# Linear attention, gated convolution and channel mixing on one core: the order of the first 40 microseconds, and eight weights' shifts moved from VectorE to ScalarE

## The chip, the cores and the metric

The kernel runs on one core of one Trainium2 chip. The metric is device time in microseconds (us), lower is better. The time before is 793.02 us, the median of three runs (792.64, 793.02 and 794.86). The engines are named as the profile names them: PE is TensorE, DVE is VectorE, ACT is ScalarE, POOL is GpSimd, SP is SyncE, which here only issues the transfers (DMAs).

## The reference

Eight sequences of 576 positions, 8 heads of 64, so rows of 512. Three stages follow each other:

```
q_s = softmax(q over its 64 features);  k_s = softmax(k over the 576 positions)
kv  = einsum('bhsd,bhde->..', k_s, v)          # 64x64 per head
x   = q_s @ kv                                  # rows of 512
gate = sigmoid(causal convolution of x, 5 taps, per channel)
x   = ((gate * (x @ w_val)) @ w_out)
xk  = mu_k*x + (1-mu_k)*x_prev;  xr = mu_r*x + (1-mu_r)*x_prev
out = sigmoid(xr @ w_r) * (relu(xk @ w_k)**2 @ w_v)
```

The five weight matrices and the convolution's taps come as float64. The kernel reads each number as two 32-bit words and makes the float32 from them.

## The kernel before, in words

The 4608 rows are handled in 12 blocks of 384. Every block runs attention (`px`), the product with w_val (`pv`), with w_out (`py`), with w_r (`racc`), with w_k (`ph`) and with w_v (`vacc`). Blocks 2 to 11 follow a fixed table; the first two blocks, the loading of all weights and the first key-value sums are issued in the order of a written list, `FRONT`. A scheduler in the framework then places the instructions of the list on each engine, so an engine's order is near to the list's but not the same; it is fixed when the program is built. Each engine works through its own queue strictly in that order.

What the front does, by the list's names:

- `lk`, `lv`, `lwval0`, ... load keys, values and weights; `qload0.0` and `qload1.0` load the two halves of the first block's query (4 heads each, tile `came`). `wval0`, `wout0`, ... turn a loaded weight chunk (tile `raw`, 128x512 pairs of words) into float32 (tile `whole`); the function is `decode`: one ACT instruction rescales the high word (L154), one DVE instruction shifts the low word right (L155), one DVE instruction joins them (L156).
- For the first key-value round: `max0` is the running maximum over the keys (tile `pm`, DVE L320 and L322); `turn0` transposes it on PE (`pmT`) and reduces it on DVE (`m1`, printed as `m`); `exp0` spreads the maximum on PE (`mx`), subtracts it (DVE, `kt`) and takes the exponential (ACT, `kt`); `vcopy0` copies the values into place (ACT, `vt`); `mm0` multiplies keys by values on PE (`kvacc`) and divides by the sums (DVE, `den`, `kvf`). `max1` to `mm1` do it for the second round, heads 4 to 7.
- `qexp0.0`, `qnorm0.0` are the softmax of the query's first half on DVE and ACT (`qm`, `qt`, `qs`); `xturn` transposes it on PE (`pq`), `xq` copies it out (ACT, `q`), `x0.0` to `x3.0` multiply it with `kvf` (PE, `px`) and copy the result (ACT, `xf`). The chunks x0 and x1 need the first half of the query and the first round, x2 and x3 the second half and the second round.
- `gate` is the convolution: one ACT and four DVE instructions for each chunk, then a tanh (ACT). `gf` multiplies it to `pv`.
- `consts` turns the convolution's taps and the mixing factors (`cwt`, `pc`, `cw`, `pm`, `mus`).
- `heat1`, `heat2`, `heat6`, `heat3`, `heat0`, `heat7` are eight transposes of the identity each on PE; nothing reads their result.

`pmT`, `mx`, `pq` and `kvacc` share the two PSUM banks of the pool `ps_t`; `pv`, `racc`, `vacc` and `heat` use the three of `ps_acc`.

Of the kernel before, what the change touches and what calls it, by code (L numbers as in the profile page):

```python
# [62 lines left out]
CONV_ON_TENSOR = ()  # L63

# [4 lines left out]
def tile_linear_attention_gated_conv_channel_mix(  # L69
# [21 lines left out]
    P = 128  # L91
# [59 lines left out]
    def decode(raw, out):  # L151

        low, high = raw[:, :, 0], raw[:, :, 1]
        nc.scalar.activation(f32(high), f32(high), AF.Prelu, scale=2.0 ** -112, alpha=2.0 ** 32)  # L154
        nc.vector.tensor_scalar(out=low, in0=low, scalar1=29, scalar2=None, op0=ALU.logical_shift_right)  # L155
        nc.vector.scalar_tensor_tensor(  # L156
            out=out.bitcast(U32), in0=high, scalar=3, in1=low, op0=ALU.logical_shift_left, op1=ALU.bitwise_or
        )
# [8 lines left out]

    cts = {}
# [9 lines left out]
    def turn_consts():  # L178
        raw, mut = cts["x"]
        t = scratch("cwt")[0:NTAP * NC, 0:P]  # L180
        decode(raw, t)
        pc = ps_t.tile([P, 512], F32, tag="t", name="pc")
        nc.tensor.transpose(pc[:, 0:NTAP * NC], t, f32(ident[0:NTAP * NC, 0:NTAP * NC]))
        nc.scalar.copy(cw, pc[:, 0:NTAP * NC])
        pm = ps_t.tile([P, 512], F32, tag="t", name="pm")
        nc.tensor.transpose(pm[:, 0:2 * NC], mut, f32(ident[0:2 * NC, 0:2 * NC]))
        ups = mus.rearrange("p x c -> p (x c)")
        nc.scalar.copy(ups[:, 0:2 * NC], pm[:, 0:2 * NC])
        nc.vector.tensor_scalar(
            out=ups[:, 2 * NC:4 * NC], in0=ups[:, 0:2 * NC], scalar1=-1.0, scalar2=1.0, op0=ALU.mult, op1=ALU.add  # L190
        )
# [28 lines left out]
    def decode_weight(n):  # L220
        w, at = CHUNKS[n]
        whole[w, at] = place(F32, "whole")
        decode(raws[n], whole[w, at])
# [50 lines left out]
    latest = {}  # L274
# [37 lines left out]
    def v_copy(st):  # L312
        nc.scalar.copy(st["v"][:, :, 0:NS4, 0:D], st["dense"])

    def kv_max(st):
        kt = st["k"]
        whole_pm = scratch("pm")
        pm = whole_pm[:, 0:HR * D]
        one = pm.rearrange("p (h d) -> p h d", d=D)
        nc.vector.tensor_max(one, kt[:, :, 0, :], kt[:, :, 1, :])  # L320
        for x in range(2, NST):
            nc.vector.tensor_max(one, one, kt[:, :, x, :])  # L322
        st["pm"] = whole_pm

    def kv_turn(st):
        pm, n = st["pm"], HR * D // P
        pmT = ps_t.tile([P, 512], F32, tag="t", name="pmT")
        for j in range(n):
            nc.tensor.transpose(pmT[:, j * P:(j + 1) * P], pm[:, j * P:(j + 1) * P], f32(ident))
        m1 = odd.tile([P, n], F32, tag="m1", bufs=2, name="m1")  # L330
        nc.vector.tensor_reduce(
            out=m1, in_=pmT[:, :n * P].rearrange("p (j t) -> p j t", j=n), axis=AX.X, op=ALU.max
        )
        st["m1"] = m1
# [33 lines left out]
    def kv_exp(st):  # L368

        kt, m1, n = st["k"], st["m1"], HR * D // P  # L370
        mx = ps_t.tile([P, 512], F32, tag="t", name="mx")
        for j in range(n):
            nc.tensor.transpose(mx[:, j * P:(j + 1) * P], m1[:, j:j + 1].to_broadcast([P, P]), f32(ident))
        nc.vector.tensor_sub(
            kt, kt, mx[:, :n * P].rearrange("p (h o d) -> p h o d", o=1, d=D).to_broadcast([P, HR, NST, D])
        )
        nc.scalar.activation(kt, kt, AF.Exp)

    def kv_mm(st):
# [3 lines left out]
        acc = ps_t.tile([P, 512], F32, tag="t", name="kvacc")  # L383
# [68 lines left out]
    def q_exp(st, h=slice(0, H)):  # L452
        n = h.stop - h.start
        qt = st["qt"][:, :, h, :]
        src = st["came"].rearrange("p h t d -> p t h d")[:, :, h, :] if "came" in st else qt
        qm = odd.tile([P, NT * n], F32, tag=f"qm{n}", bufs=1, name="qm").rearrange("p (t h) -> p t h", t=NT)
        nc.vector.tensor_reduce(out=qm, in_=src, axis=AX.X, op=ALU.max)
        nc.vector.tensor_sub(qt, src, qm.rearrange("p t (h o) -> p t h o", o=1).to_broadcast([P, NT, n, D]))
        nc.scalar.activation(qt, qt, AF.Exp)

    def q_norm(st, h=slice(0, H)):
# [136 lines left out]
    def x_chunk(st, i, c):  # L598
# [4 lines left out]
        for o, n, b, s in segs:  # L603
# [5 lines left out]
            with behind if o == 0 else nullcontext():  # L609
                passes(to, tuple(a[:, c, :] for a in kv), tuple(a[:, at] for a in st["q", c]), True, True)  # L610
        xv = padded(i, HALO, "xf", 2, "xf") if i else padded(i, HALO, "xf", NC, "xf", first)
# [8 lines left out]
        else:  # L620
            nc.scalar.copy(data, px[:, :T].rearrange("p (g t) -> p g t", g=g))
# [31 lines left out]
    def x_gate(st, i, c):  # L653
# [10 lines left out]
        nc.scalar.activation(gx(gate), data, AF.Copy, scale=tap(c, HALO))  # L664
        for sh in range(1, NTAP):
            nc.vector.scalar_tensor_tensor(  # L666
                out=gx(gate), in0=xv[:, :, HALO - sh:HALO - sh + L], scalar=tap(c, HALO - sh),
                in1=gx(gate), op0=ALU.mult, op1=ALU.add,
            )
# [11 lines left out]
    def main_steps(i, xs):  # L681
# [68 lines left out]
        def mix(c, key, mu, om, tag, pair):  # L750
# [3 lines left out]
            nc.vector.scalar_tensor_tensor(  # L754
# [135 lines left out]
    todo_front = {"cload": load_consts, "consts": turn_consts, "kvsplit": kv_split}  # L890
# [73 lines left out]
```

## Time and profile before

| | |
|---|---|
| median of three runs | 793.02 us (792.64 to 794.86) |
| the profiled execution | 793.22 us, of which the span is 791.4 us |
| PE busy in the span | 780.5 us (99%) |
| DVE busy | 600.1 us (76%) |
| ACT busy | 477.5 us (60%) |
| DMA, mean of 16 engines, 0 to 10 and 10 to 20 us | 0.79 and 1.08 |

The profile shows one execution. A timeline row is a start, a length, an engine, a source line, an operation, out<-in, sizes and how many instructions it merges; in brackets stands how long the engine sat idle before it and what released it. A product of float32 tiles is two records on PE, so `px x4` is two products. Neighbouring instructions of one engine overlap a little, so the step from start to start is often shorter than the length. `heat` and the first `pmT` stand at the start of the span, `px` at 19.02 us is the first product of the first block.

### The profile page before, as it was taken

The page shows a single profiled execution, that of the slowest core. Times are in us where ns is not written, and L with a number is a line of the kernel's source. Part 1 is how long each engine was busy: PE and PEld are TensorE (multiplying, and loading weights), DVE is VectorE, ACT ScalarE, POOL GpSimd, SP SyncE. Part 2 cuts the span into 40 slices and gives each one's busy share as a digit, 9 for nine tenths or more (in the row PEclk, how much of TensorE's full clock was granted, in tenths as well). Part 3 has the DMA queues.
Part 4 walks back from the last instruction along what each step waited for, and adds up shares of the span by engine and source line. Part 5 has one row for each costly group of instructions (what it writes and reads, how often), then busy time and mean ns, then how long its engine had stood idle before and what let it go on. Part 6 is the DMA issues. An engine that isn't in the chain of part 4 may idle for free.

```text
span 791.4 us, 12490 instructions
## 1 busy us (share of the span) xinstructions
PE 780.5 (99%) x4426; PEld 686.3 (87%) x4426; DVE 600.1 (76%) x1190; ACT 477.5 (60%) x969; POOL 64.8 (8%) x224
## 2 busy tenths in 40 slices
PE   6999999999999999999999999999999999999998
PEld 5545679999999989999999999999999999999996
DVE  7998889988788588678787678678978848755611
ACT  4667678546746665754763772763774665573542
POOL 2130001000001011100000110100000100100000
PEclk9999999999999999999999999999999999999999
DMA  9787220134133112312441411411522202101001
GB/s 314 241 273 237 60 80 1 41 104 139 35 117 102 46 46 93 89 41 82 113 100 61 128 41 48 140 37 51 141 66 82 73 15 80 59 23 39 2 1 41
DMA packets 91708, 68.88 MB, mean 87 GB/s; under 512 B 48738, under 2 KB 83454, under 8 KB 91646
## 3 DMA queue, kind: packets, MB, share of 16 engines
q1 hardware_dynamic: 91600, 68.06, 28.5%
q8 instruction: 35, 0.57, 0.3%
q14 instruction: 27, 0.22, 0.1%
q10 hardware_dynamic: 46, 0.02, 0.0%
HBM read 51.54 MB, written 16.53 MB: 86 GB/s over the span
## 4 chain that ended last, share of the span: by engine, by line
PE 95%; DMA 2%; DVE 1%; ACT 1%; SPq 1%; issue 0%; ACTq 0%
PE ph L551 26%; PE vacc L551 26%; PE racc L551 12%; PE pv L551 12%; PE py L551 12%; PE px L551 4%; PE kvacc L387 2%; DMA raw<-in_moe_w_val_dram 1%; DMA raw<-in_moe_w_k_dram 1%; DVE gate L666 1%; DMA kt<-in_k_dram 1%; PE pq L578 0%; SPq L310 0%; DVE whole L156 0%; DVE gf L717 0%; SPq L304 0%
## 5 line engine op out<-in xcount | busy, mean ns | idle before, releaser
L666 DVE SCALAR_TENSOR_TENSOR gate<-xf,cw,gate 128x384 f32<-128x384 f32 x192 | 116.3, 615 | 4.1 <-ACT gate L664 1.0
L551 PE MATMUL ph<-xkh,wk_hi 128*128 128x384 f32 x352 | 118.4, 336 | 0.0
L551 PE MATMUL ph<-xkl,wk_hi 128*128 128x384 f32 x352 | 118.2, 336 | 0.0
L551 PE MATMUL ph<-xkh,lower 128*128 128x384 f32 x352 | 117.8, 336 | 0.0
L780 ACT ACTIVATE rf<-ph 128x384 f32<-128x384 f32 x96 | 46.8, 488 | 97.9 <-PE ph L551 97.5
L544 DVE TENSOR_TENSOR kl<-rf,kh 128x384 fp32r<-128x384 f32 x88 | 48.9, 556 | 74.7 <-ACT kh L543 74.5
L551 PE MATMUL vacc<-wv_hi,kh 128*128 128x512 f32 x264 | 103.9, 394 | 0.0
L551 PE MATMUL vacc<-lower,kh 128*128 128x512 f32 x264 | 103.4, 392 | 0.0
L551 PE MATMUL vacc<-wv_hi,kl 128*128 128x512 f32 x264 | 103.3, 392 | 0.0
L543 ACT CAST gh<-gf 128x384 fp32r<-128x384 f32 x44 | 22.6, 513 | 104.0 <-DVE gf L717 104.0
L551 PEld LDWEIGHTS ph<-xkh,wk_hi 128*128 128x128 f32 x352 | 66.1, 188 | 2.4 <-ACT xkh L543 0.2
L551 PEld LDWEIGHTS ph<-xkh,lower 128*128 128x128 f32 x352 | 66.1, 188 | 2.3
L551 PEld LDWEIGHTS ph<-xkl,wk_hi 128*128 128x128 f32 x352 | 66.1, 188 | 0.0
L754 DVE SCALAR_TENSOR_TENSOR xm<-yf,mus,xm 128x384 f32<-128x384 f32 x96 | 56.2, 612 | 11.8 <-ACT xm L753 11.5
L551 PE MATMUL py<-gh,wout_hi 128*128 128x384 f32 x176 | 60.0, 341 | 0.0
L551 PE MATMUL pv<-xh,wval_hi 128*128 128x384 f32 x176 | 59.3, 337 | 0.0
L551 PE MATMUL py<-gl,wout_hi 128*128 128x384 f32 x176 | 58.9, 337 | 0.0
L551 PE MATMUL pv<-xl,wval_hi 128*128 128x384 f32 x176 | 58.9, 335 | 0.0
L551 PEld LDWEIGHTS vacc<-wv_hi,kl 128*128 128x128 f32 x264 | 49.5, 188 | 10.8 <-DVE kl L544 0.3
L551 PE MATMUL pv<-xh,lower 128*128 128x384 f32 x176 | 58.9, 334 | 0.0
L551 PE MATMUL py<-gh,lower 128*128 128x384 f32 x176 | 58.8, 336 | 0.0
L753 ACT ACTIVATE xm<-yf,mus 128x384 f32<-128x384 f32 x96 | 56.4, 615 | 3.0 <-DVE xrl L544 1.6
(152 smaller groups left out, 1696.6 us busy)
## 6 DMA issues: line engine op xcount, KB each, us to landing
out_dram<-rs SPq DMA_DIRECT2D x36, 256.0 KB, 2.2
kt<-in_k_dram SPq DMA_DIRECT2D x16, 512.0 KB, 4.4
vt<-in_v_dram SPq DMA_DIRECT2D x56, 128.0 KB, 3.9
turned<-sq SPq DMA_DIRECT2D x36, 192.0 KB, 1.9
qT<-turned SPq DMA_DIRECT2D x72, 96.0 KB, 2.2
qn<-in_q_dram SPq DMA_DIRECT2D x24, 192.0 KB, 3.4
raw<-in_moe_w_k_dram SPq DMA_DIRECT2D x8, 512.0 KB, 5.2
raw<-in_moe_w_v_dram SPq DMA_DIRECT2D x8, 512.0 KB, 5.2
```

Of the source, the lines that this page charges most:

```text
L387: nc.tensor.matmul(acc[e * D:(e + 1) * D, x * VW:(x + 1) * VW], lhsT=kt[:, 2 * x + e, s, :], rhs=st["v"][:, 2 * x + e, s, :], start=(s == ...
L543: latest["round"] = nc.scalar.copy(pair[0], a)
L544: latest["split"] = nc.vector.tensor_sub(pair[1], a, f32(pair[0]))
L551: latest["matmul"] = nc.tensor.matmul(po, lhsT=left[a], rhs=right[b], start=start and x == 0, stop=stop and x == len(m) - 1)
L666: nc.vector.scalar_tensor_tensor(out=gx(gate), in0=xv[:, :, HALO - sh:HALO - sh + L], scalar=tap(c, HALO - sh), in1=gx(gate), op0=ALU.mult ...
L753: nc.scalar.activation(gx(xf), yv[:, :, 0:L], AF.Copy, scale=om[:, c:c + 1])
L754: nc.vector.scalar_tensor_tensor(out=gx(xf), in0=yv[:, :, 1:], scalar=mu[:, c:c + 1], in1=gx(xf), op0=ALU.mult, op1=ALU.add)
L780: nc.scalar.activation(rf, ph[:, :T], AF.Relu)
```

## The change

Four things are altered, all in the first two blocks. The list `FRONT` is in another order: the first values are loaded ahead of the second keys, the constants are turned first, `max1` and `turn1` stand ahead of `xturn0.0`, and `exp1`, `wval1` and `vcopy1` ahead of `qexp1.0`. For eight weight chunks (w_val and w_out) `decode` shifts the low word on ACT instead of DVE, reading its top byte. The first round's `kvacc` and the second round's `pmT` take banks of `ps_acc` instead of `ps_t`. And many instructions are held, by `after(...)`, until a named other one in the issue order; the scheduler may not place them before it.

```diff
 FRONT = (
-    "qload.0 qload0.0 lk0 cload lwval0 lwval1 lk1 lv0 lv1 lwval2 qload1.0 lwout0 lwval3 lwout1 lwr0 max0 turn0 exp0 "
-    "lwout3 lwr1 heat1 heat2 lwout2 qexp0.0 wval0 vcopy0 mm0 heat6 qnorm0.0 heat3 heat0 heat7 xturn0.0 xq0.0 x0.0 "
-    "xturn1.0 xq1.0 x1.0 max1 qexp1.0 turn1 exp1 vcopy1 consts wval1 qnorm1.0 V0.0 mm1 gate0.0 V1.0 xturn2.0 xq2.0 "
+    "qload.0 qload0.0 lk0 cload consts lwval0 lv0 lk1 lwval1 lv1 lwval2 qload1.0 lwval3 lwout0 lwout1 lwr0 max0 turn0 "
+    "exp0 lwout3 lwr1 heat1 heat2 lwout2 qexp0.0 wval0 vcopy0 mm0 heat6 qnorm0.0 heat3 heat0 heat7 max1 turn1 xturn0.0 "
+    "xq0.0 xturn1.0 xq1.0 x0.0 exp1 wval1 x1.0 vcopy1 others qexp1.0 V0.0 mm1 qnorm1.0 gate0.0 V1.0 xturn2.0 xq2.0 "
...
+ON_SCALAR = "wval0 wval1 wval2 wval3 wout0 wout1 wout2 wout3".split()
+BEHIND = {
+    "wval0": ("mus", "m1.0"), "wval1": ("kexp.0", "m1.1"), "wval2": ("qexp.1", "kvf.1"), "wval3": ("qexp.1", "kvf.1"),
...
+        with after(act):
+            nc.scalar.activation(f32(high), f32(high), AF.Prelu, scale=2.0 ** -112, alpha=2.0 ** 32)
+            if on_scalar:
+                fourth = raw.rearrange("p n w -> p (n w)").bitcast(U8).rearrange("p (n e) -> p n e", e=8)[:, :, 3]
+                latest["shifted"] = nc.scalar.activation(low, fourth, AF.Copy, scale=2.0 ** -5, bias=-31.0 / 64)
+        with after(vec):
+            if not on_scalar:
+                nc.vector.tensor_scalar(out=low, in0=low, scalar1=29, scalar2=None, op0=ALU.logical_shift_right)
...
+    def bank_of(st, name, x):
+        if st is rounds[x]:
+            return ps_acc.tile([P, 512], F32, tag="acc", name=name)
+        return ps_t.tile([P, 512], F32, tag="t", name=name)
...
-        pmT = ps_t.tile([P, 512], F32, tag="t", name="pmT")
+        pmT = bank_of(st, "pmT", 1)
...
-        nc.vector.tensor_reduce(
-            out=m1, in_=pmT[:, :n * P].rearrange("p (j t) -> p j t", j=n), axis=AX.X, op=ALU.max
-        )
+        with after("kvf.0" if x == 1 else None):
+            latest[f"m1.{x}"] = nc.vector.tensor_reduce(
...
-        acc = ps_t.tile([P, 512], F32, tag="t", name="kvacc")
+        acc = bank_of(st, "kvacc", 0)
...
-        nc.vector.tensor_reduce(out=qm, in_=src, axis=AX.X, op=ALU.max)
+        with after("sub.1" if h.start else "cwt" if h.stop == HR else "sub.2"):
+            nc.vector.tensor_reduce(out=qm, in_=src, axis=AX.X, op=ALU.max)
```

On PE, the program's first rows before, from the identity's transposes to the first product of the first block (`m_177` and `m_320` are the first and second round's maxima, `kvf_118` the sums of sequence 0):

```order
L887 MATMUL heat<-ident 128x128 x16
L329 MATMUL pmT<-ident,pm 128x128 x2
L887 MATMUL heat<-ident 128x128 x6
L373 MATMUL mx<-ident,m_177 128x128 x2
L887 MATMUL heat<-ident 128x128 x26
L387 MATMUL kvacc<-vt,kt 64x65 x20
L578 MATMUL pq<-ident,qt 128x128 x6
L329 MATMUL pmT<-ident,pm 128x128 x2
L551 MATMUL px<-q,kvf_118 128x384 x2
```

And the same stretch of PE now (the lines have other numbers, `m_187` and `m_302` are the two maxima):

```order
L929 MATMUL heat<-ident 128x128 x2
L201 MATMUL pc<-ident,cwt 128x20
L204 MATMUL pm<-ident,mut 128x8
L929 MATMUL heat<-ident 128x128 x14
L359 MATMUL pmT<-ident,pm 128x128 x2
L405 MATMUL mx<-ident,m_187 128x128 x2
L419 MATMUL kvacc<-vt,kt 64x65 x20
L929 MATMUL heat<-ident 128x128 x32
L359 MATMUL pmT<-ident,pm 128x128 x2
L612 MATMUL pq<-ident,qt 128x128 x6
L585 MATMUL px<-q,kvf_118 128x384
```

The 32 transposes of the identity that stood ahead of `kvacc` (6 and 26) stand behind it, between it and the second round's `pmT` and the query's `pq`.

On DVE, the stretch around the second round's maximum and the query's second half before:

```order
L457 TENSOR_REDUCE qm<-came 128x12
L399 TENSOR_TENSOR kvf_118<-kvacc,den 64x2x64 x2
L458 TENSOR_TENSOR qt<-came,qm 128x3x256
L331 TENSOR_REDUCE m_320<-pmT 128x2
L155 TENSOR_SCALAR raw<-raw 128x512 x2
L374 TENSOR_TENSOR kt_125<-kt_125,mx 128x1280
L466 TENSOR_REDUCE qs<-qt 128x12
L189 TENSOR_SCALAR mus<-mus 128x8
L666 SCALAR_TENSOR_TENSOR gate<-xf,cw,gate 128x384
L467 TENSOR_SCALAR qs<-qs 128x12
```

And now:

```order
L431 TENSOR_TENSOR kvf_118<-kvacc,den 64x2x64 x2
L362 TENSOR_REDUCE m_302<-pmT 128x2
L176 SCALAR_TENSOR_TENSOR whole<-raw 128x512
L406 TENSOR_TENSOR kt_125<-kt_125,mx 128x1280
L211 TENSOR_SCALAR mus<-mus 128x8
L490 TENSOR_REDUCE qm<-came 128x12
L491 TENSOR_TENSOR qt<-came,qm 128x3x256
L705 SCALAR_TENSOR_TENSOR gate<-xf,cw,gate 128x384 x3
L426 TENSOR_SCALAR den<-kvacc 128x2
L500 TENSOR_REDUCE qs<-qt 128x12
L427 RECIPROCAL den<-den 128x2
L705 SCALAR_TENSOR_TENSOR gate<-xf,cw,gate 128x384
```

The two passes of the query's second half (`qm`, `qt`) stood ahead of the second maximum `m_320` and stand behind the subtraction `kt_125`; the sum `qs` stands behind three taps of the gate. The last pass of that half, `qt<-qt,qs`, follows seven rows further.

On ACT, from the taps' word to the copies of the query, before:

```order
L154 ACTIVATE cwraw<-cwraw 20x128
L154 ACTIVATE raw<-raw 128x512 x2
L459 ACTIVATE qt<-qt 128x3x256
L313 COPY vt<-dense 128x4x4x64
L377 ACTIVATE kt<-kt 128x1280
L313 COPY vt_126<-dense 128x4x4x64
L154 ACTIVATE raw<-raw 128x512
L590 COPY q<-pq 128x384 x2
```

And now, where L172 is the shift that came from DVE:

```order
L169 ACTIVATE cwraw<-cwraw 20x128
L202 COPY cw<-pc 128x20
L206 COPY mus<-pm 128x8
L169 ACTIVATE raw<-raw 128x512
L172 ACTIVATE raw<-raw 128x512
L335 COPY vt<-dense 128x4x4x64
L492 ACTIVATE qt<-qt 128x3x256
L409 ACTIVATE kt<-kt 128x1280
L169 ACTIVATE raw<-raw 128x512
L172 ACTIVATE raw<-raw 128x512
L624 COPY q<-pq 128x384 x2
```

One weight instead of two is decoded ahead of the first `kt`, and the copy of the second values (`vt_126`) and the third weight no longer stand ahead of the query's copies.

## Rows read from the trace of the kernel before

**Rows 1.** Page: the span; the chain that ended last, by engine.
```profile
span 791.4 us, 12490 instructions
...
PE 95%; DMA 2%; DVE 1%; ACT 1%; SPq 1%; issue 0%; ACTq 0%
```

**Rows 2.** Windows: busy per engine (instructions), granted clock, DMA share, GB/s.
```profile
20.00:30.00 10.00, 9.76 (x71) 5.77 (x70) 9.56 (x22) 8.26 (x16) 0.88 (x5) 1.00 0.71 256
30.00:40.00 10.00, 10.00 (x32) 5.61 (x31) 9.38 (x19) 5.30 (x10) 1.23 (x2) 1.00 0.77 222
...
60.00:760.00 700.00, 700.00 (x4036) 629.65 (x4035) 541.11 (x1070) 431.09 (x886) 50.59 (x177) 1.00 0.25 74
```

**Rows 3.** Timeline of PE, 0 to 60 us.
```profile
3.34 3.67 PE L887 MATMUL heat<-ident 128*128 128x128 f32 x16 [3.34 <-DVE ident L162]
9.13 0.69 PE L329 MATMUL pmT<-ident,pm 128*128 128x128 f32 x2 [2.12 <-DVE pm L322]
...
10.90 0.63 PE L373 MATMUL mx<-ident,m 128*128 128x128 f32 x2
11.32 3.67 PE L887 MATMUL heat<-ident 128*128 128x128 f32 x26
15.13 1.39 PE L387 MATMUL kvacc<-vt,kt 128*64 128x65 f32 x40
...
17.57 0.55 PE L578 MATMUL pq<-ident,qt 128*128 128x128 f32 x3 [0.57 <-ACT q L590]
...
19.02 1.56 PE L551 MATMUL px<-q,kvf 128*128 128x384 f32 x4
...
28.12 0.82 PE L578 MATMUL pq<-ident,qt 128*128 128x128 f32 x6
29.18 1.56 PE L551 MATMUL px<-q,kvf 128*128 128x384 f32 x4 [0.24 <-ACT q L590]
...
49.77 7.99 PE L551 MATMUL racc<-whole,xm 128*128 128x512 f32 x18 [0.28 <-ACT yf L745]
```

**Rows 4.** Timeline of PE, 12 to 12.5 and 13 to 13.5 us.
```profile
11.75 1.06 PE L887 MATMUL heat<-ident 128*128 128x128 f32 x4
...
12.76 0.93 PE L887 MATMUL heat<-ident 128*128 128x128 f32 x7
```

**Rows 5.** Timeline of DVE, 0 to 60 us.
```profile
8.32 0.43 DVE L155 TENSOR_SCALAR raw<-raw 128x512 uint32<-128x512 uint32 x1
8.66 0.42 DVE L322 TENSOR_TENSOR pm<-pm,kt 128x256 f32<-128x256 f32 x1
...
9.86 0.42 DVE L331 TENSOR_REDUCE m<-pmT 128x2 f32<-128x256 f32 x1
...
11.86 1.48 DVE L374 TENSOR_TENSOR kt<-kt,mx 128x1280 f32<-128x1280 f32 x1
...
17.51 0.95 DVE L457 TENSOR_REDUCE qm<-came 128x12 f32<-128x768 f32 x1
18.38 0.58 DVE L399 TENSOR_TENSOR kvf<-kvacc,den 64x128 f32<-64x128 f32 x2
...
24.86 0.95 DVE L469 TENSOR_TENSOR qt<-qt,qs 128x768 f32<-128x768 f32 x1
...
28.62 0.69 DVE L156 SCALAR_TENSOR_TENSOR whole<-raw 128x512 uint32<-128x512 uint32 x1
...
32.43 2.21 DVE L666 SCALAR_TENSOR_TENSOR gate<-xf,cw,gate 128x384 f32<-128x384 f32 x4 [0.59 <-ACT gate L664]
```

**Rows 6.** Timeline of ACT, 0 to 60 us.
```profile
8.32 0.69 ACT L154 ACTIVATE raw<-raw 128x512 f32<-128x512 f32 x1 [4.85 <-DMA raw<-in_moe_w_val_dram]
9.56 0.67 ACT L154 ACTIVATE raw<-raw 128x512 f32<-128x512 f32 x1 [0.56 <-DMA raw<-in_moe_w_val_dram]
...
13.81 1.27 ACT L377 ACTIVATE kt<-kt 128x1280 f32<-128x1280 f32 x1
...
18.15 0.48 ACT L590 COPY q<-pq 128x384 f32<-128x384 f32 x1 [0.64 <-PE pq L578]
```

More of the change, by code (lines that the diff above doesn't have):

```diff
@@ L180, in turn_consts, with other_consts @@
         t = scratch("cwt")[0:NTAP * NC, 0:P]
-        decode(raw, t)
-        pc = ps_t.tile([P, 512], F32, tag="t", name="pc")
+        latest["cwt"] = decode(raw, t)
+        pc = ps_w.tile([P, 512], F32, tag="w", name="pc")
         nc.tensor.transpose(pc[:, 0:NTAP * NC], t, f32(ident[0:NTAP * NC, 0:NTAP * NC]))
         nc.scalar.copy(cw, pc[:, 0:NTAP * NC])
-        pm = ps_t.tile([P, 512], F32, tag="t", name="pm")
+        pm = ps_w.tile([P, 512], F32, tag="w", name="pm")
         nc.tensor.transpose(pm[:, 0:2 * NC], mut, f32(ident[0:2 * NC, 0:2 * NC]))
         ups = mus.rearrange("p x c -> p (x c)")
[L188 to L191, printed above, removed]
+        latest["mus"] = nc.scalar.copy(ups[:, 0:2 * NC], pm[:, 0:2 * NC])
+    def other_consts():
+        ups = mus.rearrange("p x c -> p (x c)")
+        with after("sub.1"):
+            nc.vector.tensor_scalar(
+                out=ups[:, 2 * NC:4 * NC], in0=ups[:, 0:2 * NC], scalar1=-1.0, scalar2=1.0, op0=ALU.mult, op1=ALU.add
+            )
     def tap(c, t):
@@ L222, in decode_weight @@
         whole[w, at] = place(F32, "whole")
[L223 removed]
+        decode(raws[n], whole[w, at], n in ON_SCALAR, *BEHIND.get(n, ()))
     def open_upper():
@@ L312, in v_copy @@
     def v_copy(st):
-        nc.scalar.copy(st["v"][:, :, 0:NS4, 0:D], st["dense"])
+        with after("xf.0" if st is rounds[1] else "shifted"):
+            nc.scalar.copy(st["v"][:, :, 0:NS4, 0:D], st["dense"])
     def kv_max(st):
@@ L370, in kv_exp @@
         kt, m1, n = st["k"], st["m1"], HR * D // P
[L371 to L374, printed above, removed]
+        mx, x = ps_t.tile([P, 512], F32, tag="t", name="mx"), rounds.index(st)
+        with after("px.0" if x == 1 else None):
+            for j in range(n):
+                nc.tensor.transpose(mx[:, j * P:(j + 1) * P], m1[:, j:j + 1].to_broadcast([P, P]), f32(ident))
+        latest[f"sub.{x}"] = nc.vector.tensor_sub(
             kt, kt, mx[:, :n * P].rearrange("p (h o d) -> p h o d", o=1, d=D).to_broadcast([P, HR, NST, D])
         )
-        nc.scalar.activation(kt, kt, AF.Exp)
+        latest[f"kexp.{x}"] = nc.scalar.activation(kt, kt, AF.Exp)
     def kv_mm(st):
@@ L663, in x_gate @@
             return
-        nc.scalar.activation(gx(gate), data, AF.Copy, scale=tap(c, HALO))
+        with after("kexp.1" if i == 0 and c == 0 else None):
+            nc.scalar.activation(gx(gate), data, AF.Copy, scale=tap(c, HALO))
         for sh in range(1, NTAP):
-            nc.vector.scalar_tensor_tensor(
+            latest[f"tap.{sh}"] = nc.vector.scalar_tensor_tensor(
                 out=gx(gate), in0=xv[:, :, HALO - sh:HALO - sh + L], scalar=tap(c, HALO - sh),
@@ L716, in gated @@
             gf = one("g", 8, "gf") if i == 0 else scratch("gf")
-            nc.vector.scalar_tensor_tensor(
-                out=gf, in0=xs["gate", m], scalar=1.0, in1=pv[:, :T], op0=ALU.add, op1=ALU.mult
-            )
+            with after("tap.2" if i == 0 else None):
+                made = nc.vector.scalar_tensor_tensor(
+                    out=gf, in0=xs["gate", m], scalar=1.0, in1=pv[:, :T], op0=ALU.add, op1=ALU.mult
+                )
+            if i == 0:
+                latest[f"gf.{m}"] = made
             st["g", m] = (gf,) if i == 0 else split(gf, g_pair("g"))
```

55 lines of the change are left out of this document (33 added, 22 removed), and 7 rows, old and new, of tables (BEHIND, FRONT).

## The prediction, made before the changed kernel ran

> **What bounds the kernel now.** I read the page first. Its chain of work is 95% PE [rows 1], so a change pays only if PE loses a wait or loses work. The windows say where a wait is left: from 60 to 760 us PE is busy for 700.00 of 700 us, and DVE and ACT for 541 and 431 [rows 2]. Nothing in there can gain. PE's own timeline of the front shows the rest [rows 3]. Up to 19.02 us PE does little that counts: transposes of the identity, the small products of the first key-value round, and waits. From the first `px` at 19.02 us on it has two short waits, 0.24 us before the second `px` row and 0.28 us at `racc`, and otherwise runs without a gap. So the end of the kernel is the start of that run plus a fixed amount of PE work, plus any wait put into it. The question is when the first and the second `px` row (19.02 and 29.18 us) start in the new order. After the second one PE's order is the same as before, so I price everything at that row. What PE does in the 10.2 us between them has to be fed by a DVE that is 96% busy from 20 to 30 us [rows 2].
>
> One more reading is needed for the price. The granted-clock column says 1.00 all along [rows 2], but the transposes of the identity tell more: four from 11.75 us take 1.06 us, with 0.42 us for the last one a spacing of 0.213 us; seven from 12.76 us take 0.93 us, a spacing of 0.108 us [rows 4]. [...] So PE ran at the lower level at first, through the transposes from 3.34 us and again from 9.13 us on, and rose near 12.65 us, within the row of 26 [rows 3, 4].
>
> **The change, step by step.** First the path to `kvacc`. The shift of the first weight goes from DVE, where it stood between two `pm` passes; from its start to the next it took 0.34 us [rows 5], so the last `pm` ends at 8.74 instead of 9.08. `pmT` starts at 8.79; before, `m1` (printed `m`) started 0.73 us after it and took 0.42: it ends at 9.94. `mx` is no longer behind six transposes of the identity and starts at 9.98, 0.63 us [rows 3]. DVE joins the weight meanwhile and subtracts from 10.65 to 12.13 (1.48, [rows 5]). The exponential takes 1.27 us on ACT [rows 6]; ACT must have done the first weight (from 8.32, 0.69 us), its shift, the copy of the values and the query's exponential by then. The values now stand where the second weight stood in the DMA queue, and that one was there by 9.56 us [rows 6], so the copy is not late. `kvacc` starts at about 13.5 us instead of 15.13: 1.65 us won.
>
> Then the price of it. The 26 transposes of the identity before `kvacc` lay in a wait that PE had anyway. Now 32 of them stand behind it, ahead of `pmT` and of the query's transposes, and a queue in strict order must do them all. The query's first half is normalised by about 15 us, so they delay work that is ready. Their cost depends on the clock. PE has now paused for most of the time from 10.6 to 13.5 us, so I let `kvacc` start at the lower level: 2.65 us for what took 1.39 [rows 3], to 16.1 us. For the 32 transposes the nearest row is that of the 26 before, which also followed a pause and some 2 us of other small products and within which the clock rose: 3.67 us, 3.4 to the start of what follows [rows 3]. Six more at 0.108 are 0.65, and the end comes at 20.1 us. I call this moment E. Bounds: at the higher level from the first `kvacc` on, 1.39 + 32 x 0.108 gives E = 18.3; at the lower level to the end, 16.1 + 32 x 0.213 gives E = 22.9. I take 20.1, since that row is nearest in kind and place.
>
> From E to the first `px`: `pmT` 0.2 us at the higher level, then `pq` to the copy 0.58 us (17.57 to 18.15) and the copy, 0.48 [rows 3, 6] with two hand-overs: E + 1.35 = 21.45 us. It stood at 19.02. The wait of the query's copy on a DMA and on a free bank is gone, but behind the transposes that wins nothing.
>
> From there to the second `px` row DVE decides. `m1` of the second round can't start before `pmT`, so DVE stands still from the end of `kvf` (about 17.3 us) to E + 0.5. `mx` follows the first `px` product, and the subtraction starts at E + 2.5. Start to start, from rows 5 where a step is about 0.07 us shorter than the length: subtraction 1.4, the second half of the query 0.87 and 0.9 (these two were done ahead of the second maximum before), three taps of the gate 3 x 0.55, sum 0.87, tap 0.55, `kvf` 0.62, tap 0.55, a weight's join 0.61, the last pass 0.95, in all 9.0, and 0.6 for six small instructions and a short wait on ACT for the gate: E + 12.1. PE comes to this `pq` earlier: from `px` to `pq` it took 9.1 us before (19.02 to 28.12), less 0.35 for the constants that now go first, so E + 10.1. It waits for some 2 us. From `pq` to the second `px` row it was 1.06 us (28.12 to 29.18): E + 13.2 = 33.3 us against 29.18. That is 4.1 us later.
>
> What is hidden. The eight shifts leave DVE for 8 x 0.34 = 2.7 us, but three of them would have stood in the new idle time; the other five are why the chain above isn't longer still, and after it DVE is ahead of PE. On ACT each shift is a pass over 512 numbers that this trace doesn't show with a byte as input; nearest rows are 0.67 for the rescaling of the same size and 0.48 for a copy of 384 [rows 6], and I take 0.6. At double that, the second w_out chunk would be ready about 0.5 us after PE asks for it; at nothing, no path above is shorter, since DVE decides. Loads of later keys, values and weights move by one or two places in SP's queue and are needed 8 us or more later. The taps' decode fills DVE and PE time before the first keys are there. The 0.28 us wait at `racc` may go, or be replaced by ACT, which now decodes one more w_v chunk ahead of the first `yf`; I count it as unchanged.
>
> [...]
>
> The sum: the profiled execution took 793.22 us (span 791.4). With 4.1 us it is 797.3. It stands 0.2 us above the median of the three runs, so against the median I forecast 797.1 us. The three runs lie 2.2 us apart, and 0.3% of the time, 2.4 us, is about what can be told from no change.
>
> **Rivals.** (1) The clock rises later than I let it. The 16 transposes from 3.34 us ran at the lower level to the last, and so did all of PE's work up to 12.65 us [rows 3, 4]. Halfway between my E and none, E = 21.5, the second `px` row is at 34.7 and the sum is +5.5: 798.5; with none, +6.9: 799.9. For it speaks the pause ahead of `kvacc`, which PE didn't have ahead of the 26; against it, that `kvacc` and the 32 follow each other seamlessly. [...]
>
> (2) The clock is up at once, or DVE's chain is tighter than the rows say. With E = 18.3 the second `px` row is at 31.5, +2.3 us: 795.3, which is no change by the bound. For it: nothing in the granted-clock column speaks of a lower level. Against it: the spacing does.
>
> (3) Not slower: the transposes of the identity cost nothing. If PE reached `pmT` right behind a fast `kvacc`, E = 14.9, the chain from E gives the second `px` row at 28.1, and with the 0.28 us wait at `racc` gone the end is 1.4 us earlier: 791.6. It decides from E below 16.0, where E + 13.2 is 29.18. For it speaks that `kvacc` does come earlier; against it, that PE's rows stand in this order and 32 transposes at the higher level take 3.4 us. Only a first maximum some 2 us earlier than I work out would do it too.
>
> **Chances.** My forecast with E near 20.1: 0.48. Rival 1: 0.33. Rival 2: 0.12. Rival 3: 0.07. The first has the range 795.8 to 798.0. The range that holds 8 of 10 goes from rival 2 to most of rival 1: 794.9 to 799.4. Slower by over 0.3% needs +2.4 us: all of the forecast but its lower edge, and rival 1: 0.80. Within 0.3%: rival 2, most of rival 3 and that edge: 0.16. Faster by over 0.3%: PE's run would have to start over 2 us earlier, 0.04.
>
> **What would show it.** `kvacc` at 13.5 us, and a row of 32 `heat` right behind it that ends near 20.1 us, its first part at 0.213 us of spacing. `pmT` of the second round only then, with DVE idle for some 3 us before `m1`. The first `px` at 21.4. A wait of about 2 us on PE before the second `pq`, released by DVE's last pass over the query, and the second `px` row at 33.3. From there the same PE time as before. I am wrong if `heat` ends before 18 us, if that wait is missing, or if the second `px` row stands before 31 us; and if the row is late but the end is not, then PE had slack behind it that I took for work.

## The result, and the profile after

The changed kernel takes 800.26 us (median of six runs, 799.47 to 802.35) against 793.43 us for the kernel before (six runs, 792.64 to 794.91), a ratio of 1.0087, 95% interval 1.0070 to 1.0103. It is slower, as forecast, but by 6.8 us instead of 4.1, and the time lies above the upper end of the range, 799.4 us. The profiled execution took 801.24 us; its span is 8.0 us longer than that of before.

The page of the kernel after: span, busy time by engine, and the chain of work by engine, as in [rows 1].

```profile
span 799.4 us, 12507 instructions
...
PE 782.9 (98%) x4426; PEld 688.6 (86%) x4426; DVE 598.2 (75%) x1182; ACT 481.9 (60%) x977; POOL 64.4 (8%) x224
...
PE 90%; DVE 4%; DMA 2%; ACT 2%; issue 1%; DVEq 0%; ACTq 0%
```

PE is busy 2.4 us longer than before (780.5, with the same 4426 records) while the span grew by 8.0. So 5.6 us are more time in which it waits, and the rest is the same work at a lower granted clock (0.50 to 0.78 in the stretches listed below). PE's timeline shows where, as in [rows 3]:

```profile
8.96 0.53 PE L359 MATMUL pmT<-ident,pm 128*128 128x128 f32 x2 [0.17 <-DVE pm L346]
10.01 0.43 PE L405 MATMUL mx<-ident,m 128*128 128x128 f32 x2 [0.52 <-DVE m L362]
13.37 2.44 PE L419 MATMUL kvacc<-vt,kt 128*64 128x65 f32 x40 [2.93 <-ACT kt L409]
15.73 5.50 PE L929 MATMUL heat<-ident 128*128 128x128 f32 x32
...
22.34 0.91 PE L585 MATMUL px<-q,kvf 128*128 128x384 f32 x2 [0.24 <-ACT q L624]
...
33.07 1.51 PE L612 MATMUL pq<-ident,qt 128*128 128x128 f32 x6 [2.27 <-DVE qt L503]
34.51 2.53 PE L585 MATMUL px<-q,kvf 128*128 128x384 f32 x4
...
42.03 10.48 PE L585 MATMUL py<-gf,whole 128*128 128x384 f32 x32
53.28 1.98 PE L585 MATMUL racc<-whole,xm 128*128 128x512 f32 x4 [0.76 <-DVE xm L796]
55.80 0.70 PE L585 MATMUL racc<-whole,xm 128*128 128x512 f32 x1 [0.55 <-DVE xm L796]
```

Read it against [rows 3]. `kvacc` stands 1.76 us earlier, but takes 2.44 us for 1.39, at a granted clock of 0.50. The 32 `heat` fill PE until 21.07, and `pmT`, `pq` and the first `px` stand behind them, the last one 3.3 us later than before. Then PE waits 2.27 us for DVE's last pass over the second half of the query; the second `px` row starts 5.33 us late and takes 2.53 us for 1.56. `py` starts 6.10 us late (42.03 for 35.93). Ahead of `racc` are two waits that before had 0.28 us in one. The granted clock of PE in stretches of a microsecond, and the long run from 60 to 760 us (length, busy us, instructions, clock, DMA share, GB/s; [rows 2] has that run before, with 700.00 us busy):

```profile
13.00:14.00 1.00, 0.63 (x12) 0.50 1.11 328
18.00:19.00 1.00, 1.00 (x7) 0.50 1.04 426
19.00:20.00 1.00, 1.00 (x9) 0.78 1.03 422
33.00:34.00 1.00, 0.93 (x5) 0.54 0.83 201
37.00:38.00 1.00, 1.00 (x5) 1.00 1.16 278
60.00:760.00 700.00, 698.93 (x4013) 1.00 0.26 75
```

The granted clock was 0.50 from 13 to 19 us, after a wait of 2.93 us, and 0.50 to 0.54 again from 33 to 36 us, after the wait of 2.27. The `heat` transposes start 0.213 us apart while it is 0.50 and 0.109 us apart behind 19.5 us, with 1.00 in the column from 20 us on. These two are the lower and the higher clock of this text; where the column says 1.00 throughout, a row is put to one of them by its length. From 60 to 760 us it is no longer busy throughout: 1.07 us are missing, and the waits of PE after 60 us name them (total us, times, longest):

```profile
PE mx L405 <- DVE m L362: 0.8, 1, 0.8
PE kvacc L419 <- ACT kt L409: 0.3, 1, 0.3
```

Before had none there. They lie near 87 and 91 us, in the fourth key-value round: two splits of w_val on DVE (`lower`, 85.48 us, 1.41 us long) stand ahead of `m`; before, `m` (78.28 us) stood ahead of them. And ACT's timeline shows who holds `racc` up:

```profile
50.48 0.71 ACT L169 ACTIVATE raw<-raw 128x512 f32<-128x512 f32 x1 [2.17 <-DMA raw<-in_moe_w_v_dram]
51.06 0.49 ACT L787 ACTIVATE yf<-py 128x384 f32<-128x384 f32 x1
...
53.80 0.70 ACT L169 ACTIVATE raw<-raw 128x512 f32<-128x512 f32 x1 [0.47 <-DMA raw<-in_moe_w_k_dram]
54.38 1.12 ACT L795 ACTIVATE xm<-yf,mus 128x384 f32<-128x384 f32 x2
```

A w_v chunk stands ahead of the first `yf` in ACT's queue and waits 2.17 us for its DMA; a w_k chunk stands ahead of the second `xm` and waits again.

The 8.0 us of the two profiled executions: 5.33 at the second `px` row; 0.77 from there to `py`, with the granted clock at 0.50 up to 36 us; 0.53 from `py` to `racc` (11.25 us for 10.72) and 0.26 from there to the next `pmT` (11.21 for 10.95); 1.07 in the fourth key-value round. Sum 7.96.

### The profile page after: what moved, and what is told of

Read it like the earlier page. It is cut to its first block, busy times and chain, and to the rows that moved or that the text cites. A ratio compares the mean times of both kernels' runs of the same rounds, so it can differ in the third digit from the quotient of the medians.

```text
span 799.4 us, 12507 instructions
## 1 busy us (share of the span) xinstructions
PE 782.9 (98%) x4426; PEld 688.6 (86%) x4426; DVE 598.2 (75%) x1182; ACT 481.9 (60%) x977; POOL 64.4 (8%) x224
## 4 chain that ended last, share of the span: by engine, by line
PE 90%; DVE 4%; DMA 2%; ACT 2%; issue 1%; DVEq 0%; ACTq 0%
PE vacc L585 24%; PE ph L585 24%; PE py L585 12%; PE pv L585 11%; PE racc L585 11%; PE px L585 3%; PE kvacc L419 2%; DVE whole L176 1%; DMA raw<-in_moe_w_k_dram 1%; DMA raw<-in_moe_w_v_dram 1%; PE heat L929 1%; DMA kt<-in_k_dram 1%; ACT raw L169 1%; DVE gate L705 1%; PE pq L612 1%
## 5 line engine op out<-in xcount | busy, mean ns | idle before, releaser
L796 DVE SCALAR_TENSOR_TENSOR xm<-yf,mus,xm 128x384 f32<-128x384 f32 x96 | 56.1, 612 | 12.8 <-ACT xm L795 12.5
```

What stands on the lines that cost most here:

```text
L796: latest["mix"] = nc.vector.scalar_tensor_tensor(out=gx(xf), in0=yv[:, :, 1:], scalar=mu[:, c:c + 1], in1=gx(xf), op0=ALU.mult, op1=ALU.add)
```

## The experiments

Each stands beside runs of the kernel before on the same chip: 793.54 us for e1 to e4, 793.53 for e5, e8, e9 and e11, 793.26 for e10, e16 and e17.

**e1: no identity transposes behind `kvacc`.** The 32 are left out.

```diff
-    "... wval0 vcopy0 mm0 heat6 qnorm0.0 heat3 heat0 heat7 max1 turn1 ..."
+    "... wval0 vcopy0 mm0 qnorm0.0 max1 turn1 ..."
```

> The changed kernel without the four rows of identity transposes behind the first kvacc (32 of 48 left out, nothing else). Theory A (the 32 transposes behind kvacc delay everything by their length, and DVE's chain from the second maximum decides the second px row): kvacc at 13.4 us and at the lower clock, pq right behind it at about 15.9, the second px row at 29 to 31 us instead of 34.5; total about 796 us, 4 us under the changed kernel's 800.3. Theory B (the shift on ACT and the holds are what costs, the transposes lie in a wait that is there anyway): within 1 us of 800.3, with PE idle where the transposes stood.

Measured: 794.76 us, ratio 1.0020 (1.0009 to 1.0031). PE's timeline:

```profile
13.65 2.44 PE L419 MATMUL kvacc<-vt,kt 128*64 128x65 f32 x40 [2.93 <-ACT kt L409]
16.02 1.52 PE L612 MATMUL pq<-ident,qt 128*128 128x128 f32 x6
...
28.41 0.84 PE L612 MATMUL pq<-ident,qt 128*128 128x128 f32 x6 [2.38 <-DVE qt L503]
```

5.5 us of the 6.8 are gone. `kvacc` still takes the 2.44 us of the lower clock, and the first `pq` takes 1.52 us where it took 0.82 in the profile after, so leaving the transposes out saves the queue but not the clock. The waits ahead of `racc` shrink to 0.39 us in one, although the weight decodes stand where they stood; so what those cost hangs on the front as well.

**e2: 16 of them ahead of `kvacc`, 16 left out.**

```diff
-    "exp0 lwout3 lwr1 heat1 heat2 lwout2 ... mm0 heat6 qnorm0.0 heat3 heat0 heat7 max1 ..."
+    "heat6 heat3 exp0 lwout3 lwr1 heat1 heat2 lwout2 ... mm0 qnorm0.0 max1 ..."
```

> The changed kernel with 16 of the 32 late identity transposes issued ahead of the first mx and kvacc, in the wait for the first exponential, and the other 16 left out. Theory A: kvacc stays near 13.5 us but runs at the higher clock, the second pmT near 15.5, the second px row at about 28.5 us; total 793 to 795 us. Theory B: about 800 us.

Measured: 793.74 us, ratio 1.0004 (0.9993 to 1.0015), the time of before. PE's timeline:

```profile
14.10 1.39 PE L419 MATMUL kvacc<-vt,kt 128*64 128x65 f32 x40 [1.84 <-ACT kt L409]
...
27.87 0.85 PE L612 MATMUL pq<-ident,qt 128*128 128x128 f32 x6 [2.27 <-DVE qt L503]
28.96 1.56 PE L585 MATMUL px<-q,kvf 128*128 128x384 f32 x4 [0.24 <-ACT q L624]
```

With transposes in the gap ahead of it, `kvacc` takes the 1.39 us of the higher clock although PE waits 1.84 us. So their place is the loss. In the gap the 16 cost nothing: from DVE's first `pm` to `kvacc` it is 7.96 us in e2 and 8.22 in e1. Behind `kvacc` the 32 cost nearly their whole length: they hold PE for 5.34 us in the profile after, and without them, in e1, the second `px` row starts 5.01 us earlier. By the medians e1 is 1.0 us slower than e2, with overlapping intervals; in its profile the lower clock takes 1.05 us from `kvacc` and 0.67 from the first `pq`, and `kvacc` starts 0.45 earlier. e2 keeps all the rest of the change: the shifts, the holds, the order of the loads and the banks, to which belongs that `pc` and `pm` of the constants moved to the pool `ps_w`. What these cost and win comes to 0.2 us, with the interval above; only the shifts were also taken by themselves (e4, e5).

**e8: the kernel before, with its 32 transposes held behind `kvacc`.** The change's order without the rest of it.

```diff
-        for x in range(8):
-            nc.tensor.transpose(po[:, x % 4 * P:(x % 4 + 1) * P], f32(ident), f32(ident))
+        with tc.issue_after(latest["kvacc"].ins) if "kvacc" in latest else nullcontext():
+            for x in range(8):
+                nc.tensor.transpose(po[:, x % 4 * P:(x % 4 + 1) * P], f32(ident), f32(ident))
```

> The kernel before with one edit: its 32 identity transposes (26 + 6) that stand ahead of kvacc are held behind it, so that PE meets them ahead of pq as in the changed kernel. Theory A (late heats alone, with the lower clock that they meet, make most of the loss): kvacc at 15 us or somewhat earlier at the lower clock (2.4 us instead of 1.4), heats end near 22 us, first px near 23.5 instead of 19.0; the second px row then 1.5 to 4 us later than 29.2, since the query's second half is done early here: 795 to 798 us. Rival B (the heats cost nothing in themselves, the loss needs the new order of VectorE): 793 to 794 us.

Measured: 799.92 us, ratio 1.0084 (1.0068 to 1.0101), nearly all of the change's loss and 2 us above what I expected. PE's timeline:

```profile
14.32 2.44 PE L387 MATMUL kvacc<-vt,kt 128*64 128x65 f32 x40 [3.41 <-ACT kt L377]
16.69 4.41 PE L888 MATMUL heat<-ident 128*128 128x128 f32 x32
```

The first `px` row (22.00 us) is 3.0 us late, `py` 4.75 (40.68): the scheduler also put the second query's products apart here, with three waits of about 0.5 us, and the fourth key-value round shows the 1.1 us again. The same delay is spread in another way, so e8 shows that late transposes, with the order that the scheduler then makes, suffice for the loss, not that everything behind them is equal.

**e3 and e11: the second half of the query ahead of the second maximum**, to take away the wait of 2.27 us. The transposes stay late.

```diff
-    "... heat0 heat7 max1 turn1 ... vcopy1 others qexp1.0 V0.0 ..."
+    "... heat0 heat7 qexp1.0 max1 turn1 ... vcopy1 others V0.0 ..."
-        with after("sub.1" if h.start else "cwt" if h.stop == HR else "sub.2"):
+        with after("kvf.0" if h.start else "cwt" if h.stop == HR else "sub.2"):
```

e11 also holds the decodes that the profile blamed for `racc`:

```diff
-    "... Y3.0 lwv1 y0.0 wk1 y1.0 max2 y2.0 y3.0 lwv0 ..."
+    "... Y3.0 lwv1 y0.0 y1.0 max2 y2.0 y3.0 wk1 lwv0 ..."
-    "wv0": ("yf", "mix"),
+    "wv0": ("yf", "mix"), "wv1": ("yf", "mix"), "wk1": ("yf", "mix"),
```

> The changed kernel with the second half of the query's exponential back ahead of the second maximum (issued and held behind the first kvf instead of behind the second subtraction); the 32 transposes stay. Theory A: E stays at 21.1 us, the wait of 2.3 us on PE ahead of the second pq goes, with it the fall of the clock behind it; the second px row at about 31.5 us, total 796 to 797 us. Theory B, or if PE has slack behind that row: 799 to 800.5 us.

> The order in which the second half of the query goes ahead of the second maximum (as in the run e3, 802.5 us), and in addition the decodes of w_v chunk 1 and w_k chunk 1 stand behind the last yf on ScalarE and the mixing of the last tile on VectorE. Theory A (the 4.7 us wait of PE before racc in e3 comes from these two decodes, which wait for their DMAs in ScalarE's queue ahead of yf and xm): the wait before racc falls to under 1 us, PE's order is otherwise as in e3, the time is 802.5 - 4 to 4.7 = 797.5 to 798.5 us. Rival B (xm is late for its own reason, the py products or the yf copies): the wait stays at 4 us or more, 802 to 803 us. Rival C (the decodes become late where the w_k products need them): racc starts on time, but a wait of several us stands in the first rows that use w_k or w_v after 60 us; 800 us or more.

Measured: e3 802.5 us, ratio 1.0112 (1.0094 to 1.0130); e11 796.63 us, ratio 1.0046 (1.0030 to 1.0062). PE's and then ACT's timeline in e3:

```profile
54.13 6.22 PE L585 MATMUL racc<-whole,xm 128*128 128x512 f32 x10 [4.69 <-DVE xm L796]
```

```profile
52.14 0.68 ACT L169 ACTIVATE raw<-raw 128x512 f32<-128x512 f32 x1 [2.84 <-DMA raw<-in_moe_w_k_dram]
52.73 0.60 ACT L795 ACTIVATE xm<-yf,mus 128x384 f32<-128x384 f32 x1
```

In e3 the wait at `pq` is gone and `py` starts 3.07 us earlier, and all of it is lost again at `racc`, where a chunk of w_k waits for its DMA ahead of the first `xm`. My expectation for e3 missed that. PE's timeline in e11:

```profile
48.48 10.57 PE L585 MATMUL racc<-whole,xm 128*128 128x512 f32 x24
...
61.80 0.43 PE L405 MATMUL mx<-ident,m 128*128 128x128 f32 x2 [1.88 <-DVE m L362]
```

No wait is left at `racc`: the decodes were its cause. The time falls by 5.9 us where 4 to 4.7 were expected; the transposes end 0.97 us earlier in this profile than in that of e3. 1.88 us come back at the third maximum: on DVE `m` (61.32 us) stands behind eight passes of weight decodes from 57.55 us on, into which the held ones have moved.

**e10: the changed kernel with only these two decodes held** (e11's second diff alone).

> The changed kernel with one edit: the decodes of w_v chunk 1 and w_k chunk 1 stand behind the last yf and the last mixing pass. Theory A (the two waits of PE at racc, 0.76 and 0.55 us, come from these decodes): both under 0.4 us, the time some 0.7 us below the changed kernel's 800.3, 799 to 800 us; VectorE meets the held decodes later, so up to 1 us may come back at the third mx. Rival B (the waits at racc carry much more of the loss than the profiled execution shows, as the 4.7 us of e3): 797 us or below.

Measured: 798.60 us (797.03 to 801.33), ratio 1.0069 (1.0055 to 1.0084), 1.7 us under the changed kernel, a little below the 799 to 800 of theory A. The runs of the two overlap (799.10 to 802.35 in the ten of the changed kernel), so the size is rough. PE's timeline:

```profile
16.22 4.05 PE L929 MATMUL heat<-ident 128*128 128x128 f32 x32
...
32.11 0.85 PE L612 MATMUL pq<-ident,qt 128*128 128x128 f32 x6 [2.27 <-DVE qt L503]
33.20 1.56 PE L585 MATMUL px<-q,kvf 128*128 128x384 f32 x4 [0.24 <-ACT q L624]
...
50.43 10.57 PE L585 MATMUL racc<-whole,xm 128*128 128x512 f32 x24
```

The waits at `racc` are gone, and of those of the fourth key-value round 0.2 us is left, since DVE's order there changed too (`m` at 82.17 us, ahead of the splits). In this execution the transposes end at 20.11 us and the second `px` row stands at 33.20.

**e17: the changed kernel once more**, for a second profile.

> The changed kernel, unedited, for a second profile. Theory A (PE's clock falls when PE waits for the second pq, and this costs 1.25 us in every execution): granted clock near 0.5 from 33 to 37 us again, pq 1.5 us, 4 px 2.5 us, 800.3 us. Rival B (the fall at that place is a matter of the execution, as e2 with a wait of the same 2.27 us and no fall suggests): granted clock 1.0 there, 4 px 1.56 us, the second px row near 34 us; the median of the runs stays at 800 us and is then made of executions of both kinds.

Measured: 800.50 us, ratio 1.0089 (1.0076 to 1.0102). PE's timeline:

```profile
11.66 0.69 PE L405 MATMUL mx<-ident,m 128*128 128x128 f32 x2 [0.52 <-DMA kt<-in_k_dram]
15.28 2.44 PE L419 MATMUL kvacc<-vt,kt 128*64 128x65 f32 x40 [2.93 <-ACT kt L409]
17.64 4.28 PE L929 MATMUL heat<-ident 128*128 128x128 f32 x32
...
33.77 0.85 PE L612 MATMUL pq<-ident,qt 128*128 128x128 f32 x6 [2.27 <-DVE qt L503]
```

DVE's first `pm`, and PE's granted clock in a stretch of `kvacc`:

```profile
7.06 0.43 DVE L343 TENSOR_TENSOR pm<-kt 128x256 f32<-128x256 f32 x1 [3.32 <-DMA kt<-in_k_dram]
```

```profile
16.00:17.00 1.00, 1.00 (x24) 1.00 1.11 373
```

Rival B holds for the clock: after the same wait of 2.27 us it did not fall (1.00 in every microsecond from 33 to 37 us, and 1.56 us for the four `px`). The span is nearly as long by another way: the first keys came 1.5 us later (`pm` at 7.06 us; 5.56 in the first profile), so the transposes end at 21.77. The 7.2 us over before are 5.68 at the second `px` row, 1.26 from there to the third round's `pmT`, with waits of 0.95 and 0.84 ahead of `racc`, and 0.27 in the fourth round, where `mx` did not wait although DVE's order is that of the first profile. By the mean granted clock the ten runs of the changed kernel are of two kinds: six at 0.994 to 0.996 with a median of 800.9 us, four at 0.999 to 1.000 with 799.8. The median is made of both, and the loss is there in either.

**e4: the eight shifts back on DVE, in the new order.**

```diff
-ON_SCALAR = "wval0 wval1 wval2 wval3 wout0 wout1 wout2 wout3".split()
+ON_SCALAR = ()
```

The hold named `shifted` goes by the rescaling here.

> The changed kernel with all eight shifts back on DVE (order list, holds and banks as changed). Theory A: DVE's chain grows by one to three shifts of 0.34 us, ACT's shrinks; 0 to 1 us above 800.3, with the same 32 transposes and the same wait ahead of the second pq. Theory B: several us below 800.3, since ACT's queue ahead of yf and of the exponentials gets shorter.

Measured: 804.57 us, ratio 1.0141 (1.0125 to 1.0156). PE's and then DVE's timeline:

```profile
14.95 2.44 PE L419 MATMUL kvacc<-vt,kt 128*64 128x65 f32 x40 [3.68 <-ACT kt L409]
...
56.14 4.37 PE L585 MATMUL racc<-whole,xm 128*128 128x512 f32 x6 [3.32 <-DVE xm L796]
```

```profile
11.72 0.42 DVE L343 TENSOR_TENSOR pm<-kt 128x256 f32<-128x256 f32 x1 [0.60 <-DMA kt<-in_k_dram]
12.07 1.48 DVE L406 TENSOR_TENSOR kt<-kt,mx 128x1280 f32<-128x1280 f32 x1
```

Both theories missed: it is 4 us slower than the changed kernel, not 0 to 1 us slower nor several below. But the rows show little of the shift itself. `kvacc` is 1.58 us later: 0.93 is the first keys' transfer (`pm` starts at 6.49 us, 5.56 in the profile after), and the rest is a `pm` of the second keys that the scheduler now puts ahead of the subtraction, where it waits 0.60 us for its DMA. The wait at `racc` is 3.32 us instead of 0.76. So with the shifts elsewhere the scheduler made another order, and that order lost; the shift's own price is not isolated.

**e5: the kernel before with only the shifts on ACT.**

```diff
-        decode(raws[n], whole[w, at])
+        decode(raws[n], whole[w, at], w in ("wval", "wout"))
```

> The kernel before with only the shifts of the eight w_val and w_out chunks moved from VectorE to ScalarE (0.66 us each there, 0.34 us on VectorE). Theory A (PE sets the end, and in this order VectorE is ahead of PE except before the second px row): within 1 us of the kernel before, 792.5 to 794.5 us. Rival B (the shift on ScalarE is a gain by itself, as the 4 us between e4 and the changed kernel could suggest): 790 to 792 us. Rival C (0.66 us passes delay the query's copies on ScalarE): 795 us or more.

Measured: 797.75 us, ratio 1.0055 (1.0036 to 1.0074). DVE's and then PE's timeline:

```profile
11.53 0.95 DVE L471 TENSOR_REDUCE qs<-qt 128x12 f32<-128x768 f32 x1 [1.87 <-ACT qt L464]
12.40 0.41 DVE L336 TENSOR_REDUCE m<-pmT 128x2 f32<-128x256 f32 x1
```

```profile
13.35 4.90 PE L892 MATMUL heat<-ident 128*128 128x128 f32 x22
18.18 1.73 PE L392 MATMUL kvacc<-vt,kt 128*64 128x65 f32 x40
```

The time is that of rival C, but the chain is another than the late copies that it named. On ACT the query's exponential stands behind two shifts and starts at 10.67 us; on DVE the sum over it (`qs`) now stands ahead of `m` and waits 1.87 us for it, so `m` starts at 12.40 us (9.86 before, [rows 5]). The transposes behind `mx` then start 2 us later and 22 of them take 4.90 us where 26 took 3.67 [rows 3], and `kvacc` stands at 18.18 instead of 15.13. The change itself puts `qs` behind the subtraction (its `after("sub.0")`), so it avoids this one.

**e9 and e16: everything found, put together.** e9 joins e2, the query first and both held decodes. e16 also puts the products of tiles 2 and 3 of the query next to each other, leaves w_k chunk 1 where it was, and joins w_v 0 and 1 only behind the third maximum.

```diff
-    ("xturn2.0 xq2.0 x2.0 wval2 wval3 V2.0 xturn3.0 xq3.0 x3.0 gate1.0 ...")
+    ("xturn2.0 xq2.0 xturn3.0 xq3.0 x2.0 x3.0 wval2 wval3 V2.0 gate1.0 ...")
-    "wv0": ("yf", "mix"),
+    "wv0": ("yf", "m1.2"), "wv1": ("yf", "m1.2"),
```

> The changed kernel with three edits: two of the four late rows of identity transposes stand ahead of kvacc and two are left out (as in e2, 793.7 us), the second half of the query goes ahead of the second maximum, and the two decodes of w_v and w_k stand behind the last yf. Theory A (the three waits are independent: heats behind kvacc, VectorE before the second pq, weight decodes before racc): kvacc near 14.1 us, first px near 17.2, no wait of 2 us before the second pq (2.27 us in e2), racc wait (0.67 us in e2) under 0.4: 791 to 792.5 us, below the kernel before. Rival B (something else limits the second px row as soon as the query is no longer late, such as the first query taps or the keys' second maximum on VectorE): the wait moves to a later place before 60 us, 793.5 us or more.

> The changed kernel with all the waits that the runs so far named taken away together: 16 identity transposes ahead of kvacc and none behind it, the second half of the query ahead of the second maximum, the products of tiles 2 and 3 of the query next to each other on PE (6 pq, 4 px, 16 pv in a row; in e9 they were split and PE waited three times for 0.46 to 0.57 us), w_v chunk 1 behind the last yf and its join behind the third maximum. Theory A (the end is the start of PE's long run plus waits): kvacc near 14.1 us, px near 17.2, second pq near 26 without the 2.27 us wait of e2, py near 34 (35.9 before), no wait over 0.5 us at racc, none over 1 us at the third mx: span 1.5 to 2.5 us under the 791.4 of before, 790.8 to 792.2 us. Rival B (what is won at the front comes back as a later wait, for weights whose DMAs arrive at a fixed time): py near 34, but waits of 1.5 us or more between 46 and 100 us; 793 us or more.

Measured: e9 795.37 us, ratio 1.0029 (1.0018 to 1.0040), rival B: the second query's products were split with three waits of 0.46 to 0.57 us, and 1.96 us stood at the third maximum. e16 792.51 us (11 runs), ratio 0.9988 (0.9979 to 0.9998). PE's timeline in e16:

```profile
27.74 1.65 PE L585 MATMUL px<-q,kvf 128*128 128x384 f32 x4
...
34.53 10.53 PE L585 MATMUL py<-gf,whole 128*128 128x384 f32 x32
45.34 10.92 PE L585 MATMUL racc<-whole,xm 128*128 128x512 f32 x24 [0.28 <-DVE xm L796]
```

The span of this execution is 789.8 us, 1.6 under before, and no wait of PE is listed after 55 us. By the medians e16 is 0.75 us faster than the kernel before, 0.3 above the upper end of theory A. The interval just leaves 1 out, as one of eleven intervals here, so the new order may have something to give once the transposes are in the gap; a gain is not firmly shown.

## Why the prediction was wrong in size and right in direction

The direction and the front's mechanism held.

- **`kvacc` at 13.5 us, at the lower clock:** 13.37 us, 2.44 us long (2.65 in the sum), at a granted clock of 0.50. That the pause ahead of it would bring the lower clock was an assumption: no row that the prediction names shows a fall after a pause. The start is in part luck: the first keys came when they had come in the profile before (`pm` at 5.56 and 5.57 us), and in e17, where they came at 7.06, `kvacc` starts at 15.28.
- **32 transposes behind it hold `pmT` and `pq`:** yes; e1 takes most of the loss away by leaving them out, e2 all of it by moving half and leaving out half, and e8 makes it by moving them. Rival 3, that they cost nothing, falls.
- **From E (their end) to the rest:** first `px` E + 1.27 (E + 1.35 forecast); second `pq` E + 12.0 (E + 12.1), with PE waiting 2.27 us (about 2); second `px` row E + 13.1 in e10 and e17 (E + 13.2). In the first profile E + 13.4, since the granted clock had fallen (0.54 from 33 to 34 us).
- **The shift's price on ACT:** 0.66 to 0.69 us in the profile after (0.6 in the sum), and nothing in the sum hangs on it. What the move to ACT is worth can't be judged from these runs: e4 is slower with the shifts on DVE, e5 with them on ACT, and in both the order around them changed.

Two steps failed.

**"From there the same PE time as before."** Behind the second `px` row I counted nothing. I had named the w_v chunk that now stands ahead of the first `yf` in ACT's queue, and set it to "unchanged" without asking when its DMA lands. It waits 2.17 us there, and `yf`, `xm` and `racc` wait behind it. Nor is PE's order the same to the end: in the fourth key-value round `mx` stands behind four records of `vacc` instead of two. In the two profiles of the changed kernel what I had put at nothing measured 2.6 us (0.77, 0.53, 0.26 and 1.07 in the sum above) and 1.5 us (e17). With the decodes held (e10) the median falls by 1.7 us to 798.6, inside the range; the waits at `racc` and most of those of the fourth key-value round went together, and e10 doesn't part the two.

**The size of E.** I took 20.1 us. It was 21.07 and 21.77 in the two profiles of the changed kernel, 20.59 in e11, 21.56 in e3, and 20.11 in e10, so the term was some 1 us too small on the mean of these five (21.0). One cause is the clock. From the start of the 32 transposes to the next row it took 5.34, 4.13, 4.57, 5.38 and 3.89 us where I had 4.0: the step from one transpose to the next falls from 0.213 to 0.109 us after 17, 5, 9, 17 and 3 of them. The other is the start of `kvacc`, between 13.37 and 15.28 us with the keys' transfer. In the profile after and in e3 it is rival 1's mechanism, a later rise (E = 21.5 there), which I gave 0.33. In e17 the number fits rival 1 as well, but by luck: the 32 took nearly what I had, and the late keys moved them. Two of these five counts, 17 and 5, are from the same kernel, so the number of slow transposes differs from one execution to another. I had sized the term by one row. That row I also misread a little: in [rows 3] it is 3.81 us, not 3.4, from the 26 transposes to `kvacc`, which waited for the exponential; with the overlap that later rows show (5.50 us of length for a step of 5.34) the 26 hold PE for 3.51, so this is 0.1 us.

Of the 3.2 us between the forecast 797.1 and the 800.3 measured, 1.7 then go to the decodes and the fourth round (e10). The other 1.5 I put down to the late E; that is argued, since the one profile of e10 is of its fastest run, with E as forecast. There the span is 3.8 us over that of before, against the 4.1 forecast. What stays open is why the granted clock fell at 33 us in one execution (0.54) and not in the other (1.00), and what the shift alone is worth in an order that stays the same.

## What to carry to other kernels

Filler work on an engine with a strict queue was free here only in the gap that it filled (the 16 transposes ahead of `kvacc` in e2 cost nothing, with 7.96 us from the first `pm` to `kvacc` against 8.22 in e1; the 32 behind it held PE for 3.89 to 5.38 us); ask what stands behind it in the queue, and price it by its slowest clock, as a range over executions and not by the one row at hand. When an order changes, look in each engine's queue for instructions that wait for a DMA and now stand ahead of a short critical one: such an instruction can cost its transfer's lateness (4.69 us of PE in e3), not only its own 0.7 us. A wait taken away early shows the next one in line (e3), so removing several together (e16) is the test of whether there is a gain.

## What the runs showed of the hardware

- The granted-clock column does not show every stretch at the lower clock. In e17 `kvacc` took 2.44 us in slices where the column said 1.00; in the profile after it read 0.50 for the same length. The rows before it differ: in e17 (and e1 and e11) `mx` still took 0.69 us, so PE had not yet reached the higher clock, and the column stayed at 1.00 (for e11 by the mean of its execution, 1.000); in the profile after (and e3 and e10) `mx` took 0.43, so PE had reached it and fell again, to 0.50 in the column. In these profiles the column shows a fall, but not the lower clock that PE had from the start. The length or the spacing of equal instructions is the better witness.
- In all six profiles with a wait of 2.93 us ahead of `kvacc`, `kvacc` takes 2.43 or 2.44 us, the length of the lower clock. In three of them PE had been at the higher one and fell (after, e3, e10); in the other three it had not risen. After a wait of 1.84 us with transposes ahead of it PE kept the higher clock (e2, 1.39 us). Ahead of the second `pq` it fell after 2.27 us in one execution of the changed kernel (granted clock 0.54, six `pq` in 1.51 us), but not in the other (e17), nor in e2 and e10 with the same wait (0.85 us in all three).
- ACT's shift with a byte as input, 512 numbers read at a stride of eight bytes, takes 0.65 to 0.69 us in the rows of four profiles (after, e2, e3 and e5), about as long as the rescaling of 512 float32 (0.66 to 0.71 in the profile after).
